# A Fourier filter and a gated unit on one core: x ahead of the iotas, filters in two parts, and copy engines chosen by batch

## The chip, the cores and the metric

The kernel runs on one core of one Trainium2 chip. A core has a matrix engine (TensorE, called PE in the profile; its weight loads are PEld), VectorE (DVE), ScalarE (ACT), GpSimd (POOL) and SyncE (SP, which issues DMAs here). PE writes to PSUM; DVE and ACT copy from there to the on-chip memory. POOL issues the loads that change the type on the way, SP the stores. The metric is device time in microseconds, the median of several executions.

## The reference

The input x has 8 batches of 3200 positions and 256 channels. Each batch goes through a real Fourier transform along the positions, a product with a complex filter, and the inverse transform; the result then goes through a gated unit.

```python
X = np.fft.rfft(x, axis=1)
F = (filt_r + 1j * filt_i)[None, :, :]
x = np.fft.irfft(X * F, n=3200, axis=1)
gate_pre = sum(conv_w[k] * xp[:, k:k + S, :] for k in range(5))   # causal, xp padded by 4
gate = 1.0 / (1.0 + np.exp(-gate_pre))
out = (gate * (x @ w_val)) @ w_out
```

## The kernel before

The transform of 3200 is split into 100 times 32. For one batch the steps are: `s1`, eight pieces of matmuls of length-100 transforms over pieces of x; `S`, their copies from PSUM into a large tile `sb`; `tr1`, four transposes of `sb` on DVE, which need all eight copies; `s2`, seven pieces of length-32 transforms; `X`, their copies on ACT; `Z`, the products with the filter on DVE (`za` with the real part, `zb` with the imaginary part); `ia`, the first half of the inverse transform; `U`, its copies on ACT into the tile `ub`; `tr2`, four transposes of `ub`; `ib`, eight pieces of the second half; `Y`, their copies on ACT; then for seven chunks of positions `cv` (the convolution, as matmuls with diagonal matrices), `G` (sigmoid on ACT), `vl` (the product with `w_val`), `GV` (gate times value on DVE), `op` (the product with `w_out`), `O` (copy to an output tile) and `oi` (the store, issued by SP). A number pair such as s2 1.0 means batch 1, piece 0.

`za + zb` can be formed in two ways. Either `ia` runs its matmuls once over `za` and once over `zb` and PSUM adds (16 matmuls a full piece), or DVE adds them and `ia` runs 8. `z_engine` chooses. `s_engine` and `o_engine` choose DVE or ACT for the copies `S` and `O`.

Ahead of all this the kernel makes its tables: POOL writes counting rows (iotas), DVE computes angles from them, ACT takes sines into `cf_t` (for s1), `wf_t` (for s2), `wi_t` (for ia) and `ci_t` (for ib). The filters are loaded by POOL in 16 loads (`fload`); `t_fm` negates the imaginary part on DVE. `t_w` loads the weights, `t_wv` reorders `w_val`, `t_dg` makes the diagonals, and `t_u` sets the empty rows of both `ub` tiles to zero on POOL.

The order on each engine is fixed when the kernel is built. `pieces` lists every operation with an engine, a planned cost, what it needs and a key; the keys come from the offsets in `LAG`. `plan` then places the operations one at a time, the one that can start first, and by key where several can. The order of placement is the order of the instructions on every engine, so an operation that waits holds all that stand behind it on its engine. The costs in the plan are the author's; nothing on the chip follows them. Four PSUM tiles are shared by all matmul steps (`BUFS`, ps=4), and ten tiles hold pieces of x.

```python
def s_engine(b, j):
    return "DVE" if b < 4 and j % 4 < 2 else "ACT"
def o_engine(b, c):
    return "ACT" if c in (2, 5) else "DVE"
def z_engine(b, m):
    return "PE" if b < 7 or m in (1, 3, 5) else "DVE"
```

Lines of the profile: L486 loads x, L391 the filters, L494 is s1, L508 the transposes, L516 s2, L525 X, L533 and L537 the products, L553 ia, L563 U, L575 ib, L580 Y, L593 the convolution, L601 the sigmoid, L612 vl, L623 GV, L635 op. L480 and L482 are the copies of `S` (out `sb`) and `O` (out `o`) on ACT and DVE, L459 reorders `w_val`, L464 makes the diagonals, L473 sets `ub`'s rows.

Of the kernel before, what the change touches and what calls it, by code (L numbers as in the profile page):

```python
# [8 lines left out]
BF16 = mybir.dt.bfloat16  # L9
# [10 lines left out]
NR = 32  # L20
# [7 lines left out]
LAG = dict(x=-9.0, s2=8.36, ia=1.2, tr2=16.69, trs=0.64, ib=19.39, ibs=0.59, cv=25.03,  # L28
           vl=0.32, op=0.63, tr1=7.0)
# [15 lines left out]

F_FM = "DVE"


def pieces(L=LAG):
# [11 lines left out]
    table("t_cf", "DVE", 2.2, key=-50)  # L61
    table("t_sin", "ACT", 0.3, ["t_cf"], key=-50)
    table("t_io", "POOL", 1.8, key=-49)
    table("t_s", "DVE", 3.0, ["t_cf", "t_io"], key=-48)
    table("t_xw", "DVE", 4.6, ["t_s"], key=-47)
    table("t_wf", "ACT", 1.6, ["t_xw"], key=-46)
    table("t_wg", "ACT", 1.6, ["t_wf"], key=-46)
# [119 lines left out]
def kernel(  # L187
# [504 lines left out]
```

## Time and profile before

| | us |
|---|---|
| median of 3 executions | 347.45 (346.49 to 347.62) |
| the profiled execution | 348.45 |
| its span, from its first instruction to its last | 346.7 |
| PE busy | 301.4 (87%) |
| DVE busy | 280.7 (81%) |
| ACT busy | 267.5 (77%) |
| POOL busy | 52.2 (15%) |

The profile is of one execution. Its page gives busy time by engine, a strip of 40 slices, the chain of work that ended last, and groups of instructions by line. Answers of the trace add a timeline (start, length, engine, line, operation, tiles, count, and in brackets the idle time before it with what ended it) and windows (a stretch, its length, busy time with the number of instructions on PE, PEld, DVE, ACT and POOL, then the granted PE clock, the share of the DMA engines and GB/s). Matmuls overlap, so the start of one to the start of the next piece is the better price than their listed length.

### The profile page before, as it was taken

The numbers are of one execution on the slowest core, as the hardware profiler recorded it, in microseconds if no ns is written. First come the engines' busy times: TensorE is split into PE (matmuls) and PEld (weight loads), VectorE is DVE, ScalarE is ACT, GpSimd is POOL, SyncE is SP. The second block draws the span as 40 slices with busy tenths as digits, with TensorE's granted clock in tenths as the row PEclk, the third lists the DMA queues.
The fourth block names the chain that finished last, engine by engine and source line by source line (L and its number), as shares of the span: only waits on it lengthen the run. The fifth ranks groups of instructions, "written<-read, shape, count | busy, mean of one in ns | idle before, by whom it ended". The sixth has DMA issues, their size and how long they took to land.

```text
span 346.7 us, 8354 instructions
## 1 busy us (share of the span) xinstructions
PE 301.4 (87%) x3576; PEld 180.4 (52%) x3604; DVE 280.7 (81%) x352; ACT 267.5 (77%) x304; POOL 52.2 (15%) x112
## 2 busy tenths in 40 slices
PE   0620788788999999999999999999999999999993
PEld 0100444575566556565566556565666566567562
DVE  6957599999979887879777977888699986965574
ACT  1650488699989998999899988999898779567441
POOL 8479034102011011111111110000000000000000
PEclk9999999699999999999999999999999999999999
DMA  5999788804255656565556453122312213243244
GB/s 63 190 134 138 132 128 128 148 2 70 43 154 110 152 121 131 117 156 132 98 160 168 95 140 122 63 109 91 120 65 108 93 77 152 92 182 150 115 184 197
DMA packets 20997, 41.84 MB, mean 121 GB/s; under 512 B 4448, under 2 KB 7328, under 8 KB 20960
## 3 DMA queue, kind: packets, MB, share of 16 engines
q0 software_dynamic: 11440, 15.08, 31.1%
q1 hardware_dynamic: 9520, 26.22, 19.2%
q8 instruction: 28, 0.46, 0.6%
q14 instruction: 9, 0.07, 0.1%
HBM read 30.15 MB, written 26.21 MB: 163 GB/s over the span
## 4 chain that ended last, share of the span: by engine, by line
PE 70%; ACT 9%; DVE 8%; DMA 5%; issue 3%; POOL 3%; POOLq 0%; ACTq 0%
PE ps L593 16%; PE ps L635 13%; PE ps L553 11%; PE ps L612 11%; PE ps L516 7%; PE ps L575 6%; PE ps L494 6%; DMA xt<-in_x_dram 3%; DMA fr_t<-in_filt_r_dram 3%; ACT xs L525 2%; DVE sb L508 2%; ACT yt L580 2%; ACT ub L563 2%; ACT gt L601 1%; DVE ub L508 1%
## 5 line engine op out<-in xcount | busy, mean ns | idle before, releaser
L623 DVE TENSOR_TENSOR gv<-ps,gt 128x1024 bf16<-128x1024 f32 (+1 forms) x56 | 61.5, 1101 | 23.5 <-PE ps L612 21.7
L525 ACT ACTIVATE xs<-ps 128x1024 bf16<-128x1024 f32 (+1 forms) x56 | 53.9, 979 | 24.2 <-PE ps L516 21.8
L601 ACT ACTIVATE gt<-ps 128x1024 bf16<-128x1024 f32 (+1 forms) x56 | 52.3, 934 | 21.1 <-PE ps L593 20.5
L593 PE MATMUL ps<-yt,dg_t 64*64 64x512 bf16 (+1 forms) x1120 | 64.6, 357 | 0.5 <-ACT xs L525 0.3
L482 DVE COPY o<-ps 128x1024 f32<-128x1024 f32 (+1 forms) x40 | 44.5, 1113 | 18.5 <-PE ps L635 18.2
L480 ACT ACTIVATE sb<-ps 128x1024 bf16<-128x1024 f32 x48 | 49.6, 1041 | 12.3 <-PE ps L494 12.2
L580 ACT ACTIVATE yt<-ps 128x800 bf16<-128x800 f32 x64 | 53.8, 850 | 5.3 <-PE ps L575 4.7
L563 ACT ACTIVATE ub<-ps 128x1024 bf16<-128x1024 f32 (+1 forms) x56 | 54.5, 977 | 4.0 <-PE ps L553 3.7
L486 POOL DMA_DIRECT2D xt<-in_x_dram x64 | 35.4, 557 | 144.4 <-PE ps L494 144.3
L494 PE MATMUL ps<-xt,cf_t 100*128 100x512 bf16 x128 | 41.3, 414 | 15.5 <-DMA xt<-in_x_dram 8.3
L553 PE MATMUL ps<-za,wi_t 64*128 64x256 bf16 x416 | 49.1, 276 | 4.0 <-ACT sb L480 1.4
L635 PE MATMUL ps<-wo_t,gv 128*128 128x256 bf16 x400 | 52.6, 273 | 0.0
L516 PE MATMUL ps<-sb,wf_t 128*64 128x256 bf16 x416 | 37.0, 302 | 17.7 <-DVE sb L508 15.0
L612 PE MATMUL ps<-yt,wv_t 128*128 128x512 bf16 (+1 forms) x196 | 50.2, 354 | 1.8 <-DVE gv L623 0.4
L553 PEld LDWEIGHTS <-wi_t 64*128 64x128 f16 x804 | 38.1, 96 | 19.9 <-issue 11.3
L553 PE MATMUL ps<-zb,wi_t 64*128 64x256 bf16 x388 | 46.5, 273 | 0.0
L635 PEld LDWEIGHTS <-gv 128*128 128x128 bf16 x400 | 36.0, 98 | 14.5 <-issue 3.6
L516 PEld LDWEIGHTS <-wf_t 128*64 128x64 f16 x416 | 22.1, 116 | 37.9 <-issue 36.4
L593 PEld LDWEIGHTS <-dg_t 64*64 64x64 bf16 x1120 | 28.2, 105 | 24.9 <-issue 9.5
L533 DVE TENSOR_TENSOR za<-xs,fr_t 128x1024 bf16<-128x1024 bf16 (+1 forms) x56 | 35.6, 637 | 5.6 <-ACT xs L525 5.6
L508 DVE STREAM_TRANSPOSE ub<-ub 128x1024 uint32<-128x1024 uint32 x32 | 38.5, 1224 | 0.0
L508 DVE STREAM_TRANSPOSE sb<-sb 128x1024 uint32<-128x1024 uint32 x32 | 38.4, 1225 | 0.1
(80 smaller groups left out, 213.3 us busy)
## 6 DMA issues: line engine op xcount, KB each, us to landing
out_dram<-o SPq DMA_DIRECT2D x32, 512.0 KB, 3.0
xt<-in_x_dram POOLq DMA_DIRECT2D x64, 200.0 KB, 4.4
out_dram<-o SPq DMA_DIRECT2D x24, 384.0 KB, 2.4
fr_t<-in_filt_r_dram POOLq DMA_DIRECT2D x8, 104.0 KB, 8.0
fm_t<-in_filt_i_dram POOLq DMA_DIRECT2D x8, 104.0 KB, 5.4
yt<-in_moe_w_val_dram POOLq DMA_DIRECT2D x1, 128.0 KB, 3.7
wo_t<-in_moe_w_out_dram POOLq DMA_DIRECT2D x2, 64.0 KB, 3.5
cw<-in_moe_conv_w_dram SPq DMA_DIRECT2D x2, 2.5 KB, 3.9
```

What stands on the lines that cost most here:

```text
L494: nc.tensor.matmul(ps[:, 512 * a:512 * a + 512], lhsT=cf_t[0:NI, :], rhs=xt[0:NI, a::2, :], start=True, stop=True)
L508: nc.vector.transpose(out=w, in_=w)
L516: nc.tensor.matmul(ps[64 * h:64 * h + 64, 512 * a + D * co:512 * a + D * co + D], lhsT=wf_t[:, h, 2 * m + a, co].rearrange("p b k -> p (b ...
L525: nc.scalar.activation(xs[...].rearrange("p g c d -> p (g c d)")[:, 0:n], st.pop(("s2", b, m))[:, 0:n], AF.Copy)
L553: nc.tensor.matmul(ps[:, 512 * h + D * a:512 * h + D * a + D], lhsT=wi_t[rows, 2 * m + a, c].rearrange("p b e r -> p (b e r)"), rhs=z[rows ...
L563: nc.scalar.activation(u[:, 2 * m:2 * m + ng].rearrange("p a w c l -> p (a w) c l"), ps[:, :].rearrange("p (c w l) -> p w c l", c=2, l=2)[ ...
L580: nc.scalar.activation(y[:, :, H:H + N].rearrange("p h (i r) -> p h i r", r=NR)[:, :, :, 4 * j:4 * j + 4], st.pop(("ib", b, j))[:, :].rear ...
L593: nc.tensor.matmul(ps[64 * dh:64 * dh + 64, 512 * r:512 * r + nn], lhsT=dg_t[rows, dh, k, :], rhs=y[rows, dh, n0 + k:n0 + k + nn], start=( ...
L601: nc.scalar.activation(g[:, :, 0:nn], st.pop(("cv", b, c))[:, :].rearrange("p (h n) -> p h n", h=2)[:, :, 0:nn], AF.Sigmoid)
L612: nc.tensor.matmul(ps[:, 512 * eh:512 * eh + nn], lhsT=wv_t[:, dh, 128 * eh:128 * eh + 128], rhs=y[:, dh, H + n0:H + n0 + nn], start=(dh = ...
L623: nc.vector.tensor_tensor(gv[:, :, 0:nn].rearrange("p h (q n) -> p h q n", q=nq), st.pop(("vl", b, c))[:, :].rearrange("p (h n) -> p h n", ...
L635: nc.tensor.matmul(ps[:, D * q:D * q + D], lhsT=gv[:, eh, 128 * q:128 * q + 128], rhs=wo_t[:, eh, :], start=(eh == 0), stop=(eh == 1))
```

## The change

- POOL writes `pcol` alone first and issues two loads of x, then the `kq` iotas, two more loads, the other iotas, and the last four loads of batch 0.
- All eight `S` copies of batch 0 are on ACT; later batches have four on DVE (batch 2 has three). `O` copies and the choice for `za + zb` are listed by batch: DVE adds in pieces 1, 3, 6 of batch 0, pieces 2, 6 of batch 3 and pieces 0, 2, 3, 5, 6 of batch 7; before, it did so in pieces 0, 2, 4, 6 of batch 7.
- The filters come in two parts, groups 0 to 5 and 6 to 12, in 32 loads, and `t_fm` runs once for each part.
- `t_wv` and `t_dg` run on POOL. They, `t_w` and `t_u` come later in POOL's order.
- Scratch space of the angles lies in the two `yt` tiles (`ybig`) instead of `ub`.
- Offsets and costs of the plan are new, so the order of the instructions changes on every engine.

```diff
+FH = [(0, 6), (6, 13)]
-LAG = dict(x=-9.0, s2=8.36, ia=1.2, tr2=16.69, trs=0.64, ib=19.39, ibs=0.59, cv=25.03,
-           vl=0.32, op=0.63, tr1=7.0)
+LAG = dict(x=-12, s2=8.6, ia=1.29, tr2=16.94, trs=0.69, ib=19.57, ibs=0.59, cv=25.21, vl=0.44,
+           op=0.2, tr1=7.3, wf=-1.36, ff=6.26, wi=10, cj=7.21, ci=-10.5, tu=12, tw=8,
+           b0=-0.07, b1=-0, pc=1, pb=1)
+S_DVE = ((), (0, 2, 4, 6), (0, 3, 6), (0, 2, 4, 6), (0, 2, 4, 6), (0, 2, 4, 6), (0, 2, 4, 6),
+         (0, 2, 4, 6))
+O_ACT = ((0, 2, 4, 5), (0, 2, 4), (0, 2, 4), (0, 2, 4, 5), (0, 2, 4), (1, 4), (1, 4), (0, 2,
+         4, 5))
+Z_PE = ((0, 2, 4, 5), (0, 1, 2, 3, 4, 5, 6), (0, 1, 2, 3, 4, 5, 6), (0, 1, 3, 4, 5), (0, 1, 2,
+        3, 4, 5, 6), (0, 1, 2, 3, 4, 5, 6), (0, 1, 2, 3, 4, 5, 6), (1, 4))
 def s_engine(b, j):
-    return "DVE" if b < 4 and j % 4 < 2 else "ACT"
+    return "DVE" if j in S_DVE[b] else "ACT"
 def o_engine(b, c):
-    return "ACT" if c in (2, 5) else "DVE"
+    return "ACT" if c in O_ACT[b] else "DVE"
 def z_engine(b, m):
-    return "PE" if b < 7 or m in (1, 3, 5) else "DVE"
+    return "PE" if m in Z_PE[b] else "DVE"
...
-    for q in range(16):
-        op(("fi", 0, q), "POOL", 0.58, key=-35 + 0.01 * q)
-        op(("fd", 0, q), "DMA", 0.85, [("fi", 0, q)], key=-35 + 0.01 * q, lat=2.5)
-    table("t_fm", F_FM, 2.0 if F_FM == "DVE" else 2.9, [("fd", 0, q) for q in range(16)], key=-20)
+    for q in range(32):
+        k = -36 + 0.01 * q
+        h = FH[q // 16]
+        f = (h[1] - h[0]) / 13.0
+        op(("fi", 0, q), "POOL", 0.57, [("t_io", 0, 0)], key=k)
+        op(("fd", 0, q), "DMA", f * (1.0 if q % 2 else 0.65), [("fi", 0, q)], key=k, lat=2.5)
+    for n in range(2):
+        op(("t_fm", 0, n), "DVE", 0.6, [("fd", 0, 16 * n + q) for q in range(16)],
+           key=L["ff"] + 2 * n)
...
-    table("t_u", "POOL", 3.0, ["t_wg", "t_wj"], key=-2)
-    table("t_w", "POOL", 4.0, ["t_io"], key=-3)
-    table("t_wv", "DVE", 0.6, ["t_w"], key=-1)
-    table("t_dg", "DVE", 0.9, ["t_w"], key=-1)
+    table("t_u", "POOL", 3.0, ["t_io"], key=L["tu"])
+    table("t_w", "POOL", 3.2, ["t_io"], key=L["tw"])
+    op(("wd", 0, 0), "DMA", 1.2, [("t_w", 0, 0)], key=L["tw"], lat=3.0)
+    table("t_wv", "POOL", 1.2, [("wd", 0, 0)], key=L["tw"] + 3)
+    table("t_dg", "POOL", 1.4, [("wd", 0, 0)], key=L["tw"] + 3)
...
-    xw = scratch(ubig[1], 0, [2 * NG, 2 * NR])
-    xi = scratch(ubig[1], 6656, [NG, 4, NR])
-    wvn = scratch(ybig[1], 0, [2, D], BF16)
+    xw = scratch(ybig[0], 0, [2 * NG, 2 * NR])
+    xi = scratch(ybig[1], 0, [NG, 4, NR])
+    wvn = scratch(ybig[0], 6656, [2, D], BF16)
...
     def fload(q):
-        f, dst = ((filt_r, fr_t[...]), (filt_i, fm_t[:, :, 1, :]))[q // 8]
+        g0, g1 = FH[q // 16]
+        fi = q // 8 % 2
+        f = (filt_r, filt_i)[fi]
         u, s = (q % 8) // 2, q % 2
-        ap = [[100 * D, 16], [-D if s else D, NG], [1, D]]
-        row = 100 - 13 * u if s else 13 * u
-        nc.gpsimd.dma_start(out=dst[32 * u + 16 * s:32 * u + 16 * s + 16],
+        ap = [[100 * D, 16], [-D if s else D, g1 - g0], [1, D]]
+        row = 100 - 13 * u - g0 if s else 13 * u + g0
+        rows = slice(32 * u + 16 * s, 32 * u + 16 * s + 16)
+        nc.gpsimd.dma_start(out=fm_t[rows, g0:g1, 1] if fi else fr_t[rows, g0:g1],
...
-    def t_fm():
-        if F_FM == "DVE":
-            ts(fm_t[:, :, 0, :], fm_t[:, :, 1, :], -1.0)
-        else:
-            nc.scalar.activation(fm_t[:, :, 0, :], fm_t[:, :, 1, :], AF.Copy, scale=-1.0)
+    def t_fm(n):
+        g = slice(*FH[n])
+        ts(fm_t[:, g, 0, :], fm_t[:, g, 1, :], -1.0)
...
     def t_wv():
-            nc.vector.tensor_copy(
+            nc.gpsimd.tensor_copy(
...
     def t_dg():
-        nc.vector.tensor_tensor(
+        nc.gpsimd.tensor_tensor(
```

More of the change, by code (lines that the diff above doesn't have):

```diff
@@ L59, in table @@
            key)
-    table("t_cf", "DVE", 2.2, key=-50)
+    table("t_pc", "POOL", 0.2, key=-60)
+    table("t_kq", "POOL", 1.1, ["t_pc"], key=-37.985)
+    table("t_cf", "DVE", 1.1, ["t_kq"], key=-50)
     table("t_sin", "ACT", 0.3, ["t_cf"], key=-50)
[L63 to L67, printed above, removed]
@@ L77, in pieces @@
-    table("t_cj", "ACT", 0.3, ["t_ci"], key=-24)
-    table("t_ck", "DVE", 0.3, ["t_cj"], key=-23)
-    table("t_u", "POOL", 3.0, ["t_wg", "t_wj"], key=-2)
-    table("t_w", "POOL", 4.0, ["t_io"], key=-3)
-    table("t_wv", "DVE", 0.6, ["t_w"], key=-1)
-    table("t_dg", "DVE", 0.9, ["t_w"], key=-1)
+    table("t_io", "POOL", 1.1, ["t_kq"], key=-37.965)
+    table("t_s", "DVE", 2.4, ["t_pc"], key=-48)
+    table("t_xw", "DVE", 5.4, ["t_s", "t_io"], key=-47)
+    table("t_wf", "ACT", 1.6, ["t_xw"], key=L["wf"])
@@ new lines, in pieces @@
+    table("t_wg", "ACT", 1.6, ["t_wf"], key=L["wf"])
+    for q in range(32):
[7 more added lines that the diff above has]
+           key=L["ff"] + 2 * n)
+    table("t_q", "DVE", 2.0, ["t_s", "t_io"], key=-26)
```

55 lines of the change are left out of this document (29 added, 26 removed).

## The prediction

> **What bounds the kernel now.** First the page: the time strip, then the windows view over equal stretches, then the timeline of the start, the waits and the windows around it.
>
> ```profile
> PE   0620788788999999999999999999999999999993
> ...
> PEclk9999999699999999999999999999999999999999
> ```
>
> Each digit is 8.67 us. From the eleventh slice on TensorE (PE) is full; before that lie ten slices of ramp. The windows view (columns: stretch, length, busy us of PE, weight loads, DVE, ACT, POOL, then clock) gives both parts:
>
> ```profile
> 20.00:30.00 10.00, 1.93 (x4) 0.27 (x3) 4.01 (x3) 3.67 (x4) 9.35 (x17) 1.00 1.22 131
> 30.00:40.00 10.00, 2.93 (x28) 2.84 (x30) 7.79 (x9) 1.83 (x3) 4.25 (x8) 1.00 0.95 162
> ...
> 63.00:70.00 7.00, 5.85 (x50) 4.47 (x51) 7.00 (x10) 4.66 (x5) 0.00 (x0) 0.51 0.69 125
> ...
> 87.00:126.00 39.00, 38.01 (x479) 22.89 (x476) 34.57 (x41) 36.30 (x42) 4.53 (x9) 1.00 0.49 112
> 126.00:163.00 37.00, 36.62 (x453) 21.74 (x456) 30.37 (x35) 34.01 (x40) 4.54 (x9) 1.00 0.60 135
> ```
>
> A steady batch is 37 us, 36.6 of them PE. So two things can shorten the kernel: an earlier end of the ramp, or less PE work. The timeline of the start shows what holds the ramp:
>
> ```profile
> 3.05 4.53 POOL L486 DMA_DIRECT2D xt<-in_x_dram  x8
> 8.02 1.01 PE L494 MATMUL ps<-xt,cf_t 100*128 100x512 bf16 x2 [8.02 <-DMA xt<-in_x_dram]
> 8.26 0.52 POOL L391 DMA_DIRECT2D fr_t<-in_filt_r_dram  x1 [0.69 <-DMA xt<-in_x_dram]
> 9.60 0.59 POOL L391 DMA_DIRECT2D fr_t<-in_filt_r_dram  x1 [0.81 <-DMA xt<-in_x_dram]
> 10.69 0.50 POOL L391 DMA_DIRECT2D fr_t<-in_filt_r_dram  x1 [0.50 <-DMA xt<-in_x_dram]
> ...
> 26.13 1.14 POOL L486 DMA_DIRECT2D xt<-in_x_dram  x2
> 27.25 2.73 POOL L473 MEMSET ub<- 128x1536 bf16 x2
> 28.10 2.22 DVE L459 COPY wv_t<-yt 128x256 bf16<-128x256 bf16 x2 [5.99 <-DMA yt<-in_moe_w_val_dram]
> 29.89 4.36 POOL L486 DMA_DIRECT2D xt<-in_x_dram  x8
> ...
> 30.98 1.21 DVE L482 CAST sb<-ps 128x1024 bf16<-128x1024 f32 x1
> 32.30 4.62 DVE L508 STREAM_TRANSPOSE sb<-sb 128x1024 uint32<-128x1024 uint32 x4
> ```
>
> The eighth evacuation of batch 0's stage 1 (30.98) stands on DVE behind the copy of `w_val`, which waited 5.99 us for its load; the transposes follow and the first s2 matmul starts at 37.07. POOL's filter issues wait for x to land: every POOL load waits for the one eight issues earlier, at first 1.10 us apart (9.60, 10.69, and so on to 13.99). Batch 1 then gets to its s2 at 62.1 and batch 0 to its convolution at 86.71 over a chain of full DVE and ACT:
>
> ```profile
> 61.59 2.33 DVE L508 STREAM_TRANSPOSE ub<-ub 128x1024 uint32<-128x1024 uint32 x2
> ...
> 85.47 3.02 ACT L525 ACTIVATE xs<-ps 128x1024 bf16<-128x1024 f32 x3
> 86.71 1.27 PE L593 MATMUL ps<-yt,dg_t 64*64 64x512 bf16 x20 [0.26 <-ACT xs L525]
> ```
>
> **The change, step by step.** Times are from the span's start; the instruction order of the changed kernel is read from its list, the durations from rows of before.
>
> *Start.* pcol ends at 0.96 and x 0 is issued then, not at 3.05. From issue to first use x took 8.02-3.05 = 4.97, so x 0 is there at 5.9. At 1.10 apart x 7 lands at 13.6; by the whole of before (last x used for a wait at 16.90) at about 14.5; I take 14.0. DVE does t_s (2.5, the rows 3.14 to 5.60), t_cf (1.2), t_xw (5.8, 5.60 to 11.4), t_q, t_ci, t_xi (7.2, 11.33 to 18.57) from about 1.1: done at 17.8. All eight evacuations and one table sine are on ACT: 8 x 1.03 + 1.68 on loads 1.10 apart end near 17, so DVE's tables decide. Four transposes, 1.15 apart, end at 22.4: s2 of batch 0 starts near 22.5, 14.6 us earlier than 37.07. The copy of `w_val` and its wait are gone from this path.
>
> *Filters.* 32 loads in place of 16. POOL's issue takes 0.55 (0.54 and 0.55 by the groups). The eighth waits for x 7 (14.0); the 25 from there end at 14.0 + 25 x 0.555 = 27.9. What moving half a filter costs, the trace does not show. Above: as much as a whole one, 5.4 us median from issue to landing with eight under way, 0.68 each; below: half of that, 0.34, less than an issue. I take the issue as the pace, since bytes halve (x at twice the bytes of a whole filter load takes 1.10, so time follows size). Part A lands about 18.5 + 5 = 23.5, in time for s2; part B at 27.9 + 5 = 33, and holds groups 3 to 6 of batch 0 for that long. With the DVE work behind it (three sums and products at 1.27 or 1.96, three casts at 1.2, the last at 0.7) batch 0's products end near 43.
>
> *Batch 1's x.* POOL issues it only behind the filters: at 27.9, against 26.13 for its first two and 29.89 for the rest. So it lands from 27.9 + 4.4 (the page's median) = 32.3 on, 1.10 apart, the tenth (batch 2, piece 1) at 42.2. Here the gain is eaten: batch 1's data is no earlier than before.
>
> *A new wait.* The memsets of `ub`'s empty rows now stand behind x 2.6, and that issue waits for the load eight issues back, the tenth above: 42.2 + 0.55 + 2.73 = 45.5. The first tr2 needs the memset, and on DVE all four tr1 of batch 1 are queued behind it. By batch 0's products and the cast behind them it could have started near 43.6: about 2 us lost. From 45.6: tr2, cast, four tr1, 6 x 1.15 = 6.9; s2 of batch 1 at 52.6, against 62.1.
>
> *To the first convolution.* Before took 86.7-62.1 = 24.6, nearly all ACT: 7 X, 7 U, 8 Y, 2 S, 1 X. In the new order 1 S (1.04) and 2 X (1.02 each) more come first: 24.6 + 3.1 = 27.7, first convolution at 80.3. That is 6.4 earlier.
>
> *The work left from there.* Two ia (0.98 each, as in the chain) and one s1 (0.44) are already done: -2.4. Sums of the two products on DVE rather than as second matmuls: 2.5 whole ones more behind this point (batch 3 has 1.5, batch 7 4.5 in place of 3.5); an ia has 8 matmuls less, 0.98 against 0.54: -1.1. (Batch 0's 2.5 lie in the ramp, where PE waits.) DVE pays 0.69 for each.
>
> *Copies by batch.* From batch 4 on four S per batch go to DVE and about one O to ACT: DVE from 30.4 to 30.4 + 4 x 1.21 - 1.2 = 34.0 of 37, ACT from 34.0 to about 30.9. PE stays the bound. PE's idle time behind the first convolution sums to 3.4 in the windows; where it is told, ACT ended most. It can fall by 3.4 at most; against it, of three windows with DVE at 85 to 89% two lost 0.8 to 1.0 (one 0.3) where those at 82% lost 0.4: 0.6 more in each of four batches would be +2.4. I take -1.0, nearer the side of ACT.
>
> *Weight tables on POOL.* They stand behind x 3.7, whose buffer stage 1 of batch 2 frees, near 50 (between batch 1's transposes). Y of batch 0, at about 63, waits for the copy (it overwrites its source), the convolution at 80 for the diagonals. POOL's nearest row, 64 elements in 0.24, makes the two copies of 256 elements 1.0 each and the product of 640 elements 2.4: 4.4 in all, hidden by 8 us or more. Not hidden is the neighbour: DVE's first `w_val` copy took 2.02 and the second 0.275, the first beside POOL's memset. So POOL work can hold DVE, by up to 1.75 in that row; here transposes run beside it. I take 0, and up to +3 for the range. The Trainium skill (GPSIMD Engine Reference, 3.1) has an elementwise sum of two inputs 1.96 times as slow on POOL as on DVE; by that the diagonals take an estimated 1.6 instead of 2.4, and the sum is the same. Its table in section 1 has the two engines share their way into SBUF, for two-port modes and two inputs; by that rule the transposes would not be held, and the +3 would fall away; the row of the plain copy speaks for a hold.
>
> **Sum.** -6.4 -2.4 -1.1 -1.0 = -10.9. The profiled execution was 348.45 (span 346.7 and 1.75 around it), 1.0 above the median; against the median of 347.45 the forecast is 336.5, a span of about 335.8.
>
> **Rivals.**
>
> *Half filters cost as whole ones.* 32 x 0.68 from 14.0 ends at 35.8 with the landing of the last, batch 1's x starts landing at 37 and not 32.3, and everything behind moves 4.7: 341. For it: eight loads of only 16 partitions each; against: time follows size for x.
>
> *The memset is not late, or ACT's relief is whole.* Then 2 to 3 us more come off: 333.5. For it: ACT idles 2.6 of the 9.6 us from 62.8 in the slow-clock stretch, which need not return.
>
> *Slower: the half clock covers the ramp.* The clock was 0.51 from 63 to 70, after sparse PE work. There ACT waited 2.6 us in 9.6. In the new ramp PE has 20 us of matmuls between 52.6 and 80.3; at half clock all along they take 40, and the first convolution comes at 93, 6 later than before: 349. It takes over four stretches like the one seen (4 x 2.6 = 10.4) to cancel the gain. Against it: one stretch is all that the strip shows, in a ramp just as thin. The Trainium skill (TensorE: Matmul & The Clock Gate, part 1) has the clock fall to half after an idle window of 3.4 us and return after one of work; the trace agrees only in part: PE idled 15 us before 37.07 with a strip of 9s, but the first 32 s2 matmuls then took 3.63, 0.91 per group of eight against 0.58 later.
>
> *No change.* The ramp's gain is lost because batch 1's data is not earlier: the first convolution then stays at 86.7, the 2.4 go to DVE's waits above, and 1.1 is left: 346.3, at the edge of what can be told. Against: tr1 of batch 1 stood on DVE behind batch 0's products, which are now done.
>
> **Chances.** Forecast, 333.5 left aside, 0.52; 341 by the filters 0.15; 333.5 or lower 0.17; nothing gained 0.06; slower by the clock 0.05, by things not thought of 0.05. A change under 0.3% (1 us) can't be told from none here. Of the case with nothing gained 0.02 counts as faster. Faster 0.86, same 0.04, slower 0.10. The range runs from 331 (333.5 with the whole of PE's idle time) to 343 (341 with POOL holding DVE by 2).
>
> **What would show it.** s2's first matmul near 22.5; batch 1's first stage-1 matmul near 32; the first transpose of `ub` waiting on the POOL memset for about 2 us; s2 of batch 1 near 52.6; the first convolution near 80; DVE near 34 of 37 in steady windows with PE still full; 40 matmuls fewer on PE, with their weight loads. Wrong if: filter issues wait on filter landings for more than a few us (341), the convolution starts at 86 or later, or steady windows show PE idle over 1 us per batch with DVE as the releaser.

## The result, and the profile after

The changed kernel takes 342.58 us (median of 4 executions, 342.24 to 343.28); the kernel before, beside it, took 346.97 (4 executions, 346.49 to 347.62). The ratio is 0.9875, with a 95% interval of 0.9847 to 0.9902: faster by 4.4 us, where 336.5 was forecast. The profiled execution took 342.30, its span is 340.4. Before's profiled execution lay 1.5 above that median and this one 0.3 below its own, so the two traces differ by 6.15 where the medians differ by 4.4.

The page of the profile after, its first lines, the time strip and the shares of the chain that ended last:

```profile
PE 301.3 (88%) x3536; PEld 177.3 (52%) x3564; DVE 283.6 (83%) x358; ACT 267.7 (79%) x302; POOL 62.8 (18%) x131
PE   3636867789989999999989999899999999999994
...
PEclk9999767999999999999999999999999999999999
...
PE 64%; DVE 19%; POOL 6%; DMA 4%; issue 3%; ACT 2%; DVEq 0%; POOLq 0%; ACTq 0%
```

A digit is 8.51 us. The ramp is nine slices in place of ten and fuller, PE has 40 matmuls fewer, and yet it is busy as long as before (301.4 then). What follows the ramp is no longer solid: 8s stand in slices 12, 21 and 26, where before had none. DVE has 19% of the chain.

In the changed kernel the lines are: L508 loads of x, L516 `s1`, L502 and L504 the copies `S` and `O` on ACT and DVE, L530 the transposes, L538 `s2`, L280 `t_fm` and other scaled copies, L555, L559 and L562 the two products and their sum, L575 `ia`, L585 `U`, L615 the convolution, L623 the sigmoid, L634 `vl`, L645 `GV`, L657 `op`, L495 the zeros of `ub`, L481 and L486 the tables `t_wv` and `t_dg`. The timeline of the changed kernel's start:

```profile
17.61 4.62 DVE L530 STREAM_TRANSPOSE sb<-sb 128x1024 uint32<-128x1024 uint32 x4
22.37 5.33 PE L538 MATMUL ps<-sb,wf_t 128*64 128x256 bf16 x48 [5.90 <-DVE ci_t L280]
32.38 0.69 DVE L280 TENSOR_SCALAR fm_t<-fm_t 128x1792 bf16<-128x1792 bf16 x1 [3.43 <-DMA fm_t<-in_filt_i_dram]
33.56 0.60 PE L516 MATMUL ps<-xt,cf_t 100*128 100x512 bf16 x2 [2.37 <-DMA xt<-in_x_dram]
45.86 1.25 DVE L530 STREAM_TRANSPOSE ub<-ub 128x1024 uint32<-128x1024 uint32 x1 [2.44 <-POOL ub L495]
```

Batch 0's transposes stand directly behind its tables, and `s2` starts at 22.4, 14.7 us earlier than before. Then come two waits for loads: 3.43 us for the second part of the imaginary filter, 2.37 for batch 1's x. DVE waits 2.44 us for the zeros of `ub`.

The windows view of the changed kernel from one first convolution to the next (batches 0 to 4), columns as before:

```profile
79.70:116.80 37.10, 35.47 (x444) 21.12 (x446) 32.25 (x36) 32.97 (x38) 3.98 (x8) 1.00 0.48 118
116.80:154.20 37.40, 36.18 (x446) 21.23 (x447) 33.26 (x39) 31.94 (x37) 4.53 (x9) 1.00 0.58 134
154.20:193.10 38.90, 36.91 (x456) 21.72 (x462) 33.38 (x38) 31.62 (x36) 4.54 (x9) 1.00 0.54 128
193.10:231.90 38.80, 36.81 (x452) 21.63 (x454) 33.10 (x37) 32.22 (x37) 0.71 (x3) 1.00 0.28 96
```

Here lies the loss. An interval that took 36.9 us before takes up to 38.9, and PE idles 2.0 in each of the last two. Its waits in the changed kernel from 154 to 232 (waited for: total, times, longest) have one large entry:

```profile
PE ps L634 <- DVE sb L504: 3.6, 4, 1.2
```

PE is about to run `vl`, and waits for DVE to copy a stage-1 piece out of PSUM. DVE and then PE around one such wait, from the timeline of the changed kernel:

```profile
158.71 1.20 DVE L530 STREAM_TRANSPOSE ub<-ub 128x1024 uint32<-128x1024 uint32 x1
159.84 1.19 DVE L645 TENSOR_TENSOR gv<-ps,gt 128x1024 bf16<-128x1024 f32 x1
160.95 0.67 DVE L555 TENSOR_TENSOR za<-xs,fr_t 128x1024 bf16<-128x1024 bf16 x1
161.54 0.68 DVE L559 TENSOR_TENSOR zb<-xs,fm_t 128x1024 bf16<-128x1024 bf16 x1
162.14 1.22 DVE L504 CAST sb<-ps 128x1024 bf16<-128x1024 f32 x1
...
160.30 0.60 PE L516 MATMUL ps<-xt,cf_t 100*128 100x512 bf16 x2
160.84 0.64 PE L538 MATMUL ps<-sb,wf_t 128*64 128x256 bf16 x8
161.41 0.54 PE L597 MATMUL ps<-ci_t,ub 128*128 128x100 f16 x8
161.79 1.04 PE L657 MATMUL ps<-wo_t,gv 128*128 128x256 bf16 x8
163.41 1.02 PE L634 MATMUL ps<-yt,wv_t 128*128 128x512 bf16 x3 [0.58 <-DVE sb L504]
```

The stage-1 piece is finished by 160.9. Its copy stands on DVE behind a transpose, a `GV` and two products, and ends at 163.36. Meanwhile PE has filled the other three of the four PSUM tiles, and `vl` starts only at 163.41.

The whole stretch from the first convolution to the last `op`, in windows of before and then of the changed kernel:

```profile
sum 253.60, PE 250.12 PEld 150.77 DVE 206.28 ACT 213.55 POOL 14.52; mean PE 250.12 PEld 150.77 DVE 206.28 ACT 213.55 POOL 14.52
```

```profile
sum 254.80, PE 247.06 PEld 147.89 DVE 213.50 ACT 205.29 POOL 13.97; mean PE 247.06 PEld 147.89 DVE 213.50 ACT 205.29 POOL 13.97
```

PE has 3.06 us less to do there, but the stretch is 1.2 longer: PE's idle time grew from 3.48 to 7.74. (Both traces lack some matmul records in this stretch: before lists 3112 matmuls to 3141 weight loads, the changed kernel 3060 to 3086. So each idle time is an upper bound, and it is their difference that counts.) So the spans add up: first convolution 86.7 to 79.7, -7.0; work behind it -3.1; idle behind it +4.3; the tail behind the last `op` -0.5; together -6.3, as by the spans.

### The profile page after: what moved, and what is told of

Same layout as the page of the kernel before. It is cut to its first block, busy times and chain, and to the rows that moved or that the text cites. A ratio compares the mean times of both kernels' runs of the same rounds, so it can differ in the third digit from the quotient of the medians.

```text
span 340.4 us, 8310 instructions
## 1 busy us (share of the span) xinstructions
PE 301.3 (88%) x3536; PEld 177.3 (52%) x3564; DVE 283.6 (83%) x358; ACT 267.7 (79%) x302; POOL 62.8 (18%) x131
## 4 chain that ended last, share of the span: by engine, by line
PE 64%; DVE 19%; POOL 6%; DMA 4%; issue 3%; ACT 2%; DVEq 0%; POOLq 0%; ACTq 0%
PE ps L615 15%; PE ps L634 12%; PE ps L657 12%; PE ps L575 9%; PE ps L597 5%; PE ps L516 5%; DVE sb L530 5%; PE ps L538 5%; DMA xt<-in_x_dram 4%; DVE sb L504 3%; DVE za L555 2%; DVE ub L530 2%; DVE zb L559 2%; POOL fm_t L415 2%; DVE gv L645 2%
## 5 line engine op out<-in xcount | busy, mean ns | idle before, releaser
L645 DVE TENSOR_TENSOR gv<-ps,gt 128x1024 bf16<-128x1024 f32 (+1 forms) x56 | 61.5, 1101 | 24.3 <-PE ps L634 19.6
L623 ACT ACTIVATE gt<-ps 128x1024 bf16<-128x1024 f32 (+1 forms) x56 | 52.5, 938 | 19.6 <-PE ps L615 18.7
L585 ACT ACTIVATE ub<-ps 128x1024 bf16<-128x1024 f32 (+1 forms) x56 | 54.0, 972 | 15.3 <-PE ps L575 14.3
L615 PE MATMUL ps<-yt,dg_t 64*64 64x512 bf16 (+1 forms) x1120 | 64.4, 357 | 0.3 <-ACT gt L623 0.3
L547 ACT ACTIVATE xs<-ps 128x1024 bf16<-128x1024 f32 (+1 forms) x56 | 53.2, 968 | 8.2 <-PE ps L538 7.7
L508 POOL DMA_DIRECT2D xt<-in_x_dram x64 | 35.9, 597 | 128.1 <-PE ps L516 124.5
L516 PE MATMUL ps<-xt,cf_t 100*128 100x512 bf16 x128 | 43.4, 430 | 13.5 <-DMA xt<-in_x_dram 12.7
L634 PE MATMUL ps<-yt,wv_t 128*128 128x512 bf16 (+1 forms) x196 | 50.7, 354 | 5.0 <-DVE sb L504 3.6
L657 PE MATMUL ps<-wo_t,gv 128*128 128x256 bf16 x400 | 52.6, 273 | 0.0
L575 PE MATMUL ps<-za,wi_t 64*128 64x256 bf16 x416 | 47.8, 278 | 2.3 <-DVE sb L504 1.0
L504 DVE COPY o<-ps 128x1024 f32<-128x1024 f32 (+1 forms) x31 | 34.4, 1109 | 16.5 <-PE ps L657 16.5
L502 ACT ACTIVATE sb<-ps 128x1024 bf16<-128x1024 f32 x37 | 37.9, 1026 | 11.4 <-PE ps L516 11.0
L575 PEld LDWEIGHTS <-wi_t 64*128 64x128 f16 x764 | 34.7, 96 | 22.6 <-issue 11.8
L538 PE MATMUL ps<-sb,wf_t 128*64 128x256 bf16 x416 | 36.3, 305 | 11.3 <-DVE ci_t L280 5.9
L657 PEld LDWEIGHTS <-gv 128*128 128x128 bf16 x400 | 36.2, 98 | 13.6 <-issue 5.5
L575 PE MATMUL ps<-zb,wi_t 64*128 64x256 bf16 x348 | 41.4, 273 | 0.0
L530 DVE STREAM_TRANSPOSE ub<-ub 128x1024 uint32<-128x1024 uint32 x32 | 38.7, 1228 | 3.0 <-POOL ub L495 2.4
L615 PEld LDWEIGHTS <-dg_t 64*64 64x64 bf16 x1120 | 28.1, 105 | 23.9 <-issue 9.7
L530 DVE STREAM_TRANSPOSE sb<-sb 128x1024 uint32<-128x1024 uint32 x32 | 38.3, 1223 | 0.0
L555 DVE TENSOR_TENSOR za<-xs,fr_t 128x1024 bf16<-128x1024 bf16 (+1 forms) x56 | 35.8, 639 | 2.3 <-ACT xs L547 2.3
L538 PEld LDWEIGHTS <-wf_t 128*64 128x64 f16 x416 | 22.8, 119 | 26.3 <-issue 21.1
```

Source lines behind the costliest of these rows:

```text
L516: nc.tensor.matmul(ps[:, 512 * a:512 * a + 512], lhsT=cf_t[0:NI, :], rhs=xt[0:NI, a::2, :], start=True, stop=True)
L530: nc.vector.transpose(out=w, in_=w)
L538: nc.tensor.matmul(ps[64 * h:64 * h + 64, 512 * a + D * co:512 * a + D * co + D], lhsT=wf_t[:, h, 2 * m + a, co].rearrange("p b k -> p (b ...
L547: nc.scalar.activation(xs[...].rearrange("p g c d -> p (g c d)")[:, 0:n], st.pop(("s2", b, m))[:, 0:n], AF.Copy)
L575: nc.tensor.matmul(ps[:, 512 * h + D * a:512 * h + D * a + D], lhsT=wi_t[rows, 2 * m + a, c].rearrange("p b e r -> p (b e r)"), rhs=z[rows ...
L585: nc.scalar.activation(u[:, 2 * m:2 * m + ng].rearrange("p a w c l -> p (a w) c l"), ps[:, :].rearrange("p (c w l) -> p w c l", c=2, l=2)[ ...
```

## Experiments

The theory at the start: the ramp's gain is real, and the new copy lists lose part of it, since `S` copies on a full DVE free PSUM late. The rivals: the new offsets lose it by the order alone; or the filters in parts and the late zeros of `ub` hold the ramp. Times below are medians, and ratios go against the kernel before on the same chip (347.23 us for the first four kernels below, from again on; 347.07 for ub_early to old_plan; 347.47 for late_tables to replan_whole; 347.40 for the last two). The table has, from each profile, the first `s2` of batches 0 and 1, the first convolution (cv), the next four intervals between first convolutions, and the time from the first convolution to the last `op`.

| kernel | median | s2 0 | s2 1 | cv | intervals | cv to last op |
|---|---|---|---|---|---|---|
| before | 346.97 | 37.1 | 62.1 | 86.7 | 39.8 36.9 36.9 36.9 | 253.6 |
| changed | 342.58 | 22.4 | 52.8 | 79.7 | 37.2 37.3 38.9 38.9 | 254.8 |
| again | 342.85 | 22.4 | 52.9 | 80.1 | 37.1 37.3 38.9 38.9 | 254.8 |
| s_act | 340.39 | 22.4 | 52.7 | 81.0 | 36.6 37.5 38.2 38.1 | 252.9 |
| start_alone | 342.79 | 22.7 | 53.9 | 79.6 | 38.4 37.7 37.7 37.7 | 254.7 |
| copies_alone | 350.99 | 37.2 | 60.4 | 84.9 | 41.1 37.7 38.6 38.5 | 258.0 |
| ub_early | 341.06 | 22.4 | 52.0 | 78.9 | 37.2 37.3 38.9 38.9 | 254.8 |
| filters_whole | 338.57 | 22.6 | 48.1 | 75.0 | 37.1 37.4 38.9 38.9 | 254.9 |
| old_lag | 341.17 | 23.4 | 54.9 | 80.5 | 39.2 36.9 36.9 37.1 | 253.8 |
| old_plan | 339.64 | 22.4 | 53.1 | 77.0 | 39.7 36.9 36.9 37.1 | 253.7 |
| late_tables | 339.85 | 28.4 | 53.5 | 77.8 | 39.8 36.9 36.9 36.9 | 253.7 |
| old_plan_whole | 335.10 | 22.4 | 49.2 | 73.0 | 39.7 36.9 36.9 36.9 | 253.5 |
| old_plan_whole_ub | 335.14 | 22.4 | 48.2 | 72.1 | 39.7 36.9 36.9 36.9 | 253.5 |
| replan_whole | 340.19 | 22.4 | 52.9 | 78.6 | 39.5 36.9 36.9 36.9 | 253.3 |
| s_list_alone | 354.67 | 36.9 | 59.9 | 84.4 | 41.8 38.8 38.8 38.8 | 261.8 |
| o_list_alone | 347.47 | 37.2 | 61.7 | 86.0 | 39.7 36.2 37.1 37.8 | 253.8 |

The first convolution is less certain than the intervals. Up to it the kernels changed, again and s_act have the same order on every engine, and it comes at 79.7, 80.1 and 81.0; the same holds for before and o_list_alone, with 86.7 and 86.0. A difference of about 1 us in that column, in a single profile, tells nothing by itself.

### The changed kernel again

> The changed kernel once more, beside the kernel before on the same chip: 342.6 again (ratio near 0.9875), by every theory. It is the base for the others of this group.

Measured 342.85, ratio 0.9865 (0.9829 to 0.9902). The intervals agree to 0.1 with the first profile, so a change of 0.7 us in an interval, below, belongs to the kernel.

### The S copies of batches 4 to 7 on ACT, the order kept

```diff
-        copy(s_engine(b, j),
+        copy("ACT" if b >= 4 else s_engine(b, j),
```

> Changed kernel, order of all instructions kept, but the S copies of batches 4 to 7 (four per batch on DVE) go to ACT at the same place. Theory (a stage-1 copy queued on DVE behind transposes, gate products and filter products holds one of the four PSUM tiles, and PE waits for it): the waits of vl for the S copy, 0.6 and 1.2 us twice per batch interval, go; the intervals between first convolutions of 38.9 and 38.8 come back to near 37, and the time falls by 3 to 4 us to about 339. Rival (ACT at 32 of 38.8 us is not free either, with 4 us more per batch its own copies come late): the waits change their releaser from DVE to ACT and the time stays within 1 us of 342.6. Second rival (the intervals are long because of the new order of PE's instructions, whoever copies): no change of the intervals.

Measured 340.39, ratio 0.9802 (0.9764 to 0.984), 2.5 below the changed kernel beside it (the stretch from the first convolution to the last `op`, which the edit bears on, is 1.9 shorter). The windows of two intervals, and PE's three largest waits in them:

```profile
155.00:231.30 76.30, 74.52 (x910) 44.02 (x908) 57.95 (x67) 70.07 (x82) 5.25 (x12) 1.00 0.42 114
```

```profile
PE ps L575 <- ACT xs L547: 0.8, 2, 0.4
PE ps L634 <- ACT gt L623: 0.6, 2, 0.3
PE ps L575 <- ACT sb L502: 0.4, 2, 0.2
```

The waits of `vl` for DVE (3.6 us) are gone, and the intervals fall from 38.9 to 38.2 only. ACT is now busy 70.07 of 76.3 and the waits are for ACT. So the copies on DVE cost something, but they are not the whole loss.

### The new start with the old copy lists

```diff
-S_DVE = ((), (0, 2, 4, 6), (0, 3, 6), (0, 2, 4, 6), (0, 2, 4, 6), (0, 2, 4, 6), (0, 2, 4, 6),
-         (0, 2, 4, 6))
...
+S_DVE = ((),) + ((0, 1, 4, 5),) * 3 + ((),) * 4
+O_ACT = ((2, 5),) * 8
+Z_PE = ((0, 1, 2, 3, 4, 5, 6),) * 7 + ((1, 3, 5),)
```

> The new start, filters in two parts, weight tables on GpSimd and all offsets as in the changed kernel, but the lists of copy engines hold the old choices (S of batch 0 still all on ACT, batches 1 to 3 pieces 0, 1, 4, 5 on DVE, later ones on ACT; O 2 and 5 on ACT; sums on DVE in batch 7's pieces 0, 2, 4, 6). Theory: the ramp gain stays (first convolution near 80, 7 us earlier) and the steady intervals are 37 again: about 338 to 340. Rival (the order by the new offsets loses the time): intervals near 38 to 39 and 342 to 344.

Measured 342.79, ratio 0.9866 (0.9825 to 0.9906): no better than the changed kernel, a miss for the theory. The later three intervals are 37.7, each 0.8 over those of before, with the same copies on the same engines. What is left of the change in these batches is the order, by the new offsets and planned costs. PE has one listed wait in two intervals (155 to 231):

```profile
PE ps L631 <- ACT o L499: 0.8, 2, 0.4
```

`vl` waits for an `O` copy on ACT. That is 0.4 of the 0.8 in each interval; for the rest no single wait is listed.

### The new copy lists in the kernel before

```diff
+S_DVE = ((0, 1, 4, 5), (0, 2, 4, 6), (0, 3, 6), (0, 2, 4, 6), (0, 2, 4, 6), (0, 2, 4, 6), (0, 2, 4, 6),
+         (0, 2, 4, 6))
...
-    return "DVE" if b < 4 and j % 4 < 2 else "ACT"
+    return "DVE" if j in S_DVE[b] else "ACT"
...
-    return "ACT" if c in (2, 5) else "DVE"
+    return "ACT" if c in O_ACT[b] else "DVE"
...
-    return "PE" if b < 7 or m in (1, 3, 5) else "DVE"
+    return "PE" if m in Z_PE[b] else "DVE"
```

Batch 0 keeps its old choices; the order is planned by the old offsets and costs.

> The kernel before with its old start, plan and offsets, and of the change only the lists of copy engines (batch 0's rows left as they were). Theory: PE does about 1.1 us less work, but DVE's S copies in batches 4 to 7 cost waits of about 4 us in the intervals: 348 to 351, slower than before. Rival (the lists are neutral or a gain by themselves, the loss comes only with the new order): 345 to 347.

Measured 350.99, ratio 1.009 (1.0059 to 1.0121). The lists alone make the kernel slower: 4.4 us more from the first convolution to the last `op`, although `Z` takes work from PE.

### The zeros of ub on DVE, earlier

```diff
-            nc.gpsimd.memset(u[:, NG:16], 0.0)
+            nc.vector.memset(u[:, NG:16], 0.0)
...
+            if (kind, j) == ("t_fm", 1):
+                t_u()
```

> Changed kernel, order kept, but the zeroing of ub's empty rows is done by DVE while it waits for the second part of the filters (before the second negation), not by POOL behind the x loads. Theory (the POOL memset, 2.44 us of DVE idle before the first tr2 at 45.9, sits on the path to batch 1's s2 and on to the first convolution): s2 of batch 1 from 52.8 to about 50.5, first convolution from 79.7 to about 77.5, time 2 us less, about 340.5. Rival (behind the memset something else is as late, for example ACT's copies of U or the x pieces of batch 2): s2 of batch 1 moves less than 1 us and the time by less than 1.

Measured 341.06, ratio 0.9829 (0.9808 to 0.9851). The first transpose of `ub` starts at 45.09 instead of 45.86 and no longer waits for POOL, but `s2` of batch 1 and the first convolution come only 0.8 earlier. In this profile most of the 2.44 us of waiting was not the memset's to give back: the zeros now take 1.50 us of DVE, and its copies in front of the transpose wait 0.85 and 0.89 for stage 1, where in the changed kernel they waited 0.23 in all. Those waits lie in a stretch of half clock that here lasted from 34.3 to 41.1, and in the changed kernel from 35.2 to 38.6, so they need not come of the edit. The median is 1.5 to 1.8 below that of the changed kernel; how much of the 2.44 the memset really costs, between 0.8 and that, stays open.

### The filters in 16 whole loads, the order kept

```diff
-        g0, g1 = FH[q // 16]
+        g0, g1 = 0, NG
...
-        g = slice(*FH[n])
+        g = slice(0, NG)
...
+            if kind == "fi" and j > 15 or (kind, j) == ("t_fm", 1):
+                continue
```

> Changed kernel, order kept, but the filters come in 16 whole loads and are negated once. Theory (POOL's issue time of 0.55 per load, not the bytes, sets when batch 1's x is issued; 16 loads fewer are 8.8 us of issues): batch 1's first stage-1 matmul from 33.6 to about 28, batch 0's first product from 24.5 to about 28 (it now waits for all filters), s2 of batch 1 about 3 us earlier at 50, first convolution about 77, time about 2.5 us less. Rival (halves pay: products start later and the whole of batch 0 with them): s2 of batch 1 no earlier, time equal or up to 3 us more.

Measured 338.57, ratio 0.9768 (0.9735 to 0.9801): 4.0 us below the changed kernel. Two rows of POOL and one of DVE, from this kernel's timeline:

```profile
21.94 2.75 POOL L508 DMA_DIRECT2D xt<-in_x_dram  x5 [0.28 <-DMA fm_t<-in_filt_i_dram]
38.55 2.71 POOL L495 MEMSET ub<- 128x1536 bf16 x2
...
25.55 1.09 DVE L280 TENSOR_SCALAR fm_t<-fm_t 128x3328 bf16<-128x3328 bf16 x1 [2.93 <-DMA xt<-in_x_dram]
```

Batch 1's x is issued at 21.94, where the changed kernel issues it at 28.47; it lands at 27.3 against 33.5. The whole filter is there at 25.4, against 32.3 for the second part. The price is a later first product (26.6 against 24.5), which by the fourth piece is won back (30.9 against 33.0). Stage 1 of batch 1 itself starts only 1.6 earlier (31.9; 28 was expected), as in the kept order it stands on PE behind the first products, which now come later. From there on its pieces of x are ready, and `s2` of batch 1 comes 4.7 earlier (48.1 against 52.8), as does the first convolution. So the parts of the filter cost this kernel 4.7 us of its ramp.

### The new start with the old offsets, then with the old planned costs too

Both go on from the new start with the old lists. The first puts back the ten old offsets:

```diff
-LAG = dict(x=-12, s2=8.6, ia=1.29, tr2=16.94, trs=0.69, ib=19.57, ibs=0.59, cv=25.21, vl=0.44,
-           op=0.2, tr1=7.3, wf=-1.36, ff=6.26, wi=10, cj=7.21, ci=-10.5, tu=12, tw=8,
+LAG = dict(x=-9.0, s2=8.36, ia=1.2, tr2=16.69, trs=0.64, ib=19.39, ibs=0.59, cv=25.03,
+           vl=0.32, op=0.63, tr1=7.0, wf=-1.36, ff=6.26, wi=10, cj=7.21, ci=-10.5, tu=12, tw=8,
```

> As start_alone (new start, old lists of copy engines), and with the ten offsets that both kernels have at their old values; planned costs are the new ones. Theory (the new offsets order PE's work so that PE waits 0.8 us more in a batch interval, 37.7 against 36.9): intervals of 36.9 to 37.0 between first convolutions, first convolution near 80, about 339.5. Rival (the planned PE costs, now lower than the chip's, make the order): intervals stay near 37.7 and the time near 342.5.

The second also puts back what the plan charges for PE's steps (`s1` 0.45 for 0.44, `s2` 0.46 for 0.43, `vl` 0.92 for 0.88, `op` 0.92 for 0.89, and):

```diff
-            op(("ib", b, j), "PE", 0.38, [("tr2", b, p) for p in range(4)] +
+            op(("ib", b, j), "PE", 0.46, [("tr2", b, p) for p in range(4)] +
...
-            op(("ia", b, m), "PE", (0.42 if add else 0.82) * f, [("Z", b, m), ("t_wj", 0, 0)], key=k,
+            op(("ia", b, m), "PE", (0.46 if add else 0.92) * f, [("Z", b, m), ("t_wj", 0, 0)], key=k,
...
-            op(("cv", b, m), "PE", 1.05 * f, [("Y", b, j) for j in range(8)] +
+            op(("cv", b, m), "PE", 1.15 * f, [("Y", b, j) for j in range(8)] +
```

> As old_lag, and with the planned PE costs of the batch loop at their old values too. By the theory of the offsets it equals old_lag, 339 to 340. By the rival of the planned costs, here and not in old_lag the intervals come back to 36.9: about 339.5 against 342.5. If both keep 37.7, neither offsets nor costs make the order, but what the earlier start leaves in the queues.

Measured 341.17 (0.9838, 0.9809 to 0.9868) and 339.64 (0.9789, 0.9762 to 0.9817). With the old offsets the steady intervals are 36.9 to 37.1 again: the 0.8 was the order's. The first kernel misses its 339.5 all the same, for its first convolution comes at 80.5. With the old costs everything behind the first convolution is before's to 0.1, while the first convolution comes at 77.0. So the new start is worth 9.7 us there, and the new offsets, costs and lists together give 2.7 of that back ahead of the first convolution and 1.2 behind it. Which of the ten offsets does it was not tried.

### One move alone in the kernel before: w_val and the diagonals behind batch 0's transposes

```diff
+            if kind in ("t_wv", "t_dg"):
+                continue
...
+            if (kind, b, j) == ("tr1", 0, 3):
+                t_wv()
+                t_dg()
```

> The kernel before, with one move: the copy of w_val and the diagonals on DVE stand behind the four transposes of batch 0 instead of ahead of its last stage-1 copy. Theory (that wait of 5.99 us is what held batch 0; batch 1's x is the later limit): s2 of batch 0 from 37.1 to about 29.5, but batch 1's first stage-1 matmul stays near 33 to 40 and s2 of batch 1 gains about 4 us; first convolution about 82, time about 4 us less, 343. Rival (the wait is covered, the memset, filters or x of batch 1 decide): within 1 us of before.

Measured 339.85, ratio 0.9789 (0.9767 to 0.981): -7.6 us, more than the whole change, by moving two table steps on the same engine. The timeline of DVE in this kernel:

```profile
18.54 4.61 DVE L482 CAST sb<-ps 128x1024 bf16<-128x1024 f32 x4
23.61 4.62 DVE L508 STREAM_TRANSPOSE sb<-sb 128x1024 uint32<-128x1024 uint32 x4 [0.46 <-ACT sb L480]
28.15 1.68 DVE L459 COPY wv_t<-yt 128x256 bf16<-128x256 bf16 x2
```

The transposes start at 23.61 instead of 32.30, and by the time the copy comes its load has landed. It was a miss in size, since 4 us were expected: the whole 8.7 us reach the first convolution (86.7 to 77.8), as batch 1's work behind it on DVE moves too. (In this profile the clock was full from 32.0 on, where in before it was at half from 63 to 70, so a part of that can be the clock's; by the medians it is 7.6.)

### The best of both, and two variants

The new start, old lists, old plan and whole filters, that is old_plan with the edit of filters_whole:

```diff
-        g0, g1 = FH[q // 16]
+        g0, g1 = 0, NG
```

> old_plan (new start, old lists, offsets and planned costs) and 16 whole filter loads with one negation, order kept. Theory (the two gains are in different places, the ramp by the loads and the steady intervals by the order): first convolution from 77.0 to about 73, intervals 39.7, 36.9, 36.9, 37.1 as in old_plan, about 336. Rival (with the old order the ramp is held elsewhere, for example by DVE's stage-1 copies of batch 1): no more than 1 us under old_plan's 339.6.

The same with the zeros of `ub` on DVE ahead of `t_fm`:

```diff
-            nc.gpsimd.memset(u[:, NG:16], 0.0)
+            nc.vector.memset(u[:, NG:16], 0.0)
...
+            if (kind, j) == ("t_fm", 0):
+                t_u()
```

> As old_plan_whole, with ub's empty rows zeroed by DVE ahead of the negation. ub_early alone brought 0.8 us at the first convolution; if that holds here, 335; if the memset is off the path by now, equal to old_plan_whole.

And whole filters that the planner knows of, so that the order is planned anew:

```diff
-FH = [(0, 6), (6, 13)]
+FH = [(0, 13)]
...
-    for q in range(32):
+    for q in range(16):
```

> old_plan with the 16 whole loads known to the plan, so that the order is made for them. Theory: as old_plan_whole or up to 2 us better, 334 to 336. Rival (the new order happens to put copies badly, as the new offsets did): intervals over 37.5 and no better than 338.

Measured 335.10 (0.9648, 0.9626 to 0.9671), 335.14 (0.965, 0.9623 to 0.9677) and 340.19 (0.9806, 0.978 to 0.9833). The first is 12.4 us faster than before and some 7.5 faster than the changed kernel; its windows from the second first convolution on are those of before:

```profile
112.80:149.70 36.90, 36.73 (x456) 21.66 (x455) 30.26 (x35) 33.91 (x40) 4.54 (x9) 1.00 0.59 135
149.70:186.60 36.90, 36.73 (x455) 21.68 (x454) 30.27 (x35) 33.92 (x40) 4.54 (x9) 1.00 0.58 135
```

The zeros on DVE move the first convolution by 0.9 and the median not at all. The new order is a miss: stage 1 of batch 1 starts earlier (28.0) but `s2` of batch 1 at 52.9, 3.7 later. Of that, DVE and POOL of this kernel show:

```profile
36.17 0.69 DVE L552 TENSOR_TENSOR za<-xs,fr_t 128x1024 bf16<-128x1024 bf16 x1 [2.76 <-PE ps L572]
39.36 1.22 DVE L501 CAST sb<-ps 128x1024 bf16<-128x1024 f32 x1 [1.90 <-PE ps L513]
42.83 2.04 DVE L552 TENSOR_TENSOR za<-xs,fr_t 128x512 bf16<-128x512 bf16 x1
44.80 0.41 DVE L556 TENSOR_TENSOR zb<-xs,fm_t 128x512 bf16<-128x512 bf16 x1
...
42.62 0.74 POOL L478 COPY wv_t<-yt 128x256 bf16<-128x256 bf16 x2
43.33 1.25 POOL L483 TENSOR_TENSOR dg_t<-ident,cw 128x640 bf16<-128x640 f32 x1
```

DVE idles 2.76 and 1.90 behind PE where steps of batch 1 were put ahead of batch 0's, and a product that takes 0.41 took 2.04 beside POOL's tables.

### The lists one by one in the kernel before

Each has the lists of copies_alone, but only one of the three functions reads its list: `s_engine` in the first, `o_engine` in the second.

```diff
-    return "DVE" if b < 4 and j % 4 < 2 else "ACT"
+    return "DVE" if j in S_DVE[b] else "ACT"
```

> The kernel before with only the list of the S copies (batches 1 to 7 as in the change; O copies and product sums old). Theory (the S copies on DVE in batches 4 to 7 are what costs in copies_alone): intervals of the third and fourth batch at 38 or more against 36.9, time 348 to 351. Rival (the O copies on ACT cost): intervals near 36.9 and time within 1 us of before. DVE would hold 35 of 37 us here, as O stays with it, so it can be worse than copies_alone's 351.

```diff
-    return "ACT" if c in (2, 5) else "DVE"
+    return "ACT" if c in O_ACT[b] else "DVE"
```

> The kernel before with only the list of the O copies. Theory: ACT gets about one copy more per batch (35 of 37), DVE less; intervals 36.9 to 37.3, time 347 to 348. Rival: if the O copies are what costs in copies_alone, 349 to 351.

Measured 354.67 (1.0228, 1.0201 to 1.0254) and 347.47 (1.0003, 0.9984 to 1.0022). Two steady batches and PE's largest wait from 126 to 243, with the `S` list:

```profile
163.00:240.00 77.00, 73.81 (x904) 43.29 (x904) 68.58 (x77) 61.20 (x70) 5.79 (x13) 1.00 0.42 114
```

```profile
PE ps L524 <- DVE sb L490: 3.7, 3, 1.2
```

DVE is at 89%, each interval is 1.9 longer, and PE again waits for a stage-1 copy; the step held is `s2` here (L524). The slowdown is more than the 348 to 351 expected. The `O` list alone moves nothing. So the `S` list is the harmful one, by 7.3 us; with `O` and `Z` beside it (copies_alone, 3.8 over before) 3.5 of these are won back. The `Z` list alone was not run. In all three kernels the order is planned anew for the list, so that it too differs from before's; only s_act changes the copies and nothing else.

## Why the prediction was right and wrong

The sign was right, and 342.58 lies just inside the range, but the forecast missed by 6.1 us. About 4.8 of it is in the terms: -10.9 forecast, -6.15 between the profiled executions. The other 1.3 is how profile and median stand: the changed kernel's median was taken to lie 1.0 below its profiled execution, as before's did, and lay 0.3 above it. The terms, against the spans:

| term | forecast | traces |
|---|---|---|
| first convolution | -6.4 | -7.0 |
| work already done, sums on DVE | -3.5 | -3.1 |
| copies by batch, PE idle behind the first convolution | -1.0 | +4.3 |
| tail behind the last `op` | none | -0.5 |

**Start: right.** `s2` of batch 0 at 22.4 (22.5 forecast), stage 1 of batch 1 at 33.6 (32 to 32.3), a wait of 2.44 for the zeros (2), `s2` of batch 1 at 52.8 (52.6), the first convolution at 79.7 (80.3). The first part of the filter landed at 22.4 and the second at 32.3 (23.5 and 33).

**Half filters as dear as whole ones: no.** The issue paced them, as taken. But the prediction treated the split as given and asked only whether x came later than hoped; filters_whole shows that sixteen whole loads would have had x there 6 us earlier. It wrote that "batch 1's data is no earlier than before" and did not price how much of that the split adds.

**The memset: right as a wait, smaller as a cost.** The rival gave 2 to 3 us for its absence; ub_early shows 0.8 by its profile and 1.5 to 1.8 by its medians.

**The weight tables on POOL at 0: right here.** POOL took 0.40 for each copy of `w_val` and 1.25 for the diagonals, 2.0 in all where 4.4 were forecast, and the cast and the transposes beside them on DVE kept their times:

```profile
52.34 0.74 POOL L481 COPY wv_t<-yt 128x256 bf16<-128x256 bf16 x2
53.05 1.25 POOL L486 TENSOR_TENSOR dg_t<-ident,cw 128x640 bf16<-128x640 f32 x1
...
52.66 1.18 DVE L504 CAST sb<-ps 128x1024 bf16<-128x1024 f32 x1
53.77 2.35 DVE L530 STREAM_TRANSPOSE ub<-ub 128x1024 uint32<-128x1024 uint32 x2
```

The hold that the upper end of +3 allowed for exists: replan_whole shows 1.6 where a product lies there instead.

**The clock: more of it, and not free.** The windows at half clock in the changed kernel:

```profile
35.20:38.60 3.40, 3.40 (x25) 1.67 (x26) 3.40 (x5) 2.48 (x3) 3.03 (x7) 0.50 1.03 187
45.40:55.70 10.30, 7.05 (x36) 2.89 (x38) 9.84 (x9) 4.82 (x5) 8.53 (x14) 0.50 1.01 181
```

They are 13.7 us, twice those of before (63 to 70). In the longer one DVE was busy 9.84 of 10.30 and PE 7.05, so PE was hardly what set the pace there. Later in the ramp it is. Here is one stretch of the changed kernel, and the same of s_act, which has the same order there and in whose profile the clock fell once more:

```profile
69.60:73.00 3.40, 3.22 (x44) 2.21 (x43) 3.40 (x5) 3.40 (x5) 1.10 (x2) 1.00 0.40 52
69.60:73.00 3.40, 3.40 (x28) 1.99 (x27) 2.21 (x4) 2.72 (x4) 0.55 (x1) 0.50 0.39 45
```

From 47 to 70 ACT's copies in the two traces run within 0.1 us of each other. In this stretch PE then starts 28 matmuls in place of 44, and behind it everything is 1.3 later, the first convolution too (81.0 against 79.7). Eight executions of the changed kernel say the same: the span is 340.2 where the mean clock was 0.980, and 342.0 where it was 0.966. These 1.8 us go with 9.5 us more at half clock (2 x 0.014 x 341), and by that rate an estimate for the 13.7 us is 2.6. Before shows no such trend (35 executions, clock 0.985 to 1.0, spans 344.3 to 347.1). So the rival was right that the half clock returns in the new ramp, but by this estimate it costs 2 to 3 us, not the 12.5 (349 against 336.5) of its price.

**The step that failed** is "Copies by batch", put as "I take -1.0, nearer the side of ACT". It weighed DVE's and ACT's busy shares, got DVE about right (34.0 forecast, 33.1 to 33.4 in the windows), and set PE's idle time by how full ACT would be. Even its upper bound (+2.4) was too low: PE idles 4.3 us more. What the runs showed in its place has two parts. The `S` copies on DVE: PE waits for a PSUM tile whose copy stands in DVE's queue (3.6 of the 3.8 us by which two intervals of the changed kernel are longer than before's; s_list_alone, +1.9 an interval; s_act, where taking these copies off DVE gave 2.5 us). And the order, which the prediction costed at nothing: the new offsets take 0.8 an interval with the copies unchanged (start_alone 37.7, old_lag 36.9). The two do not add up. From the first convolution to the last `op`, the new lists cost 4.4 us under the old offsets (copies_alone, 258.0 against 253.6) and 0.1 under the new ones (changed, 254.8 against start_alone's 254.7), although they take work from PE. So the new order helps the new lists, and either way the stretch is longer than before's. The prediction's own sign of error, PE idle over 1 us a batch with DVE as the releaser, is what the windows and waits show.

**A gain not asked for.** The first term was forecast from the whole of the new start. With the old lists and plan it is worth 9.7 us at the first convolution, and late_tables shows that one move, that of `t_wv` and `t_dg`, gives 8.9 without the rest of it; with whole filters the new start gives 13.7 (73.0).

**Where the order's time goes.** The starts of PE's matmuls show it. In two steady intervals each of before, old_lag, start_alone, s_act and the changed kernel, the time from one matmul to the next within a step sums to 52.2 to 52.5 us, the same in all. What differs is the time at the 101 or 102 places where PE goes from one step to another: 21.1, 21.5, 23.0, 23.6 and 25.1 us. So it is lost at the changes of step, in waits and in costlier successions of steps, and that is why s_act's intervals stay at 38.2 and PE is listed as busy for 37.3 of it, against 36.6 before. Open: which offset does the harm.

## What to carry to other kernels

On an engine with a fixed order, look first for an operation that waits for a load with others ready behind it: moving it behind them was worth 2.1% here, more than the whole change. A PSUM copy put on another engine is to be priced by where it stands in that engine's queue and by who needs the tile next, not by the engine's busy share. And a load cut in two is two issues: where the issue sets the pace, everything behind it in that queue comes later.

## What the runs showed of the hardware

Going from one step to another costs PE more where the weights change their shape. In before, the first matmul of `ib` (128x128 weights) starts 0.11 us behind the last of `op` (128x128), and the first of `cv` (64x64) 0.20; behind `ib`, `op` starts after 0.04 and `ia` (64x128) after 0.14. That is some 0.095 us a change. In two steady intervals start_alone has 74 such changes and before 71, which makes an estimated 0.3 of the 1.5 us between them.

POOL can hold some of DVE's work, but not all of it. A product of two inputs took 2.04 instead of 0.41 beside POOL's copy and product (replan_whole), while the cast from PSUM and the 32-bit transposes beside the same POOL work kept their 1.18 and about 1.2 (changed kernel). The Trainium skill (SBUF — State Buffer, SBUF: two separate sides) has VectorE and GpSimd share a pair of ports under an exclusive lock, and VectorE need it for two-port modes, or for two inputs in SBUF against a GpSimd operation that reads SBUF. The trace agrees: the held operation had two such inputs, and POOL was reading.

Loads with half the bytes did not come at half the distance: POOL's issue took 0.5 to 0.6 us whatever the size, and the last of 32 halves landed at 32.3 where the last of 16 whole ones landed at 25.4.
